# Transformer block on one core: last chunk's sum kept in SBUF, a new order of the turned steps, other queues and banks

## The chip, the core and the metric

The kernel runs on one core of a Trainium2 chip. A core has TensorE (PE) for matrix products, VectorE (DVE), ScalarE (ACT) and GpSimd (POOL) for the rest, and SyncE (SP), which here only issues DMAs. Each engine works through its own list of instructions in order; they meet through semaphores. Matmuls write into the eight banks of PSUM; everything else lives in SBUF or, through DMAs, in device memory. The metric is the time of one execution in microseconds (us).

## The reference

The input is one sequence of 2048 tokens with 448 features. An attention part with 16 heads of width 28, but one common key and one common value head, and an MLP part of width 1792 both read the input, and their results are added to it:

```python
xn = _layernorm(x)
# A: q = (xn @ wq) in 16 heads; k = xn @ wk; v = xn @ wv   (one head each)
#    p = softmax(q k^T * 28**-0.5);  A = (p v) @ wo
# B: y = _layernorm(xn);  B = gelu(y @ w1 + b1) @ w2 + b2
return x + A + B
```

All of it is in float32. The kernel keeps that precision on TensorE by splitting operands into a high and a low part and adding the products.

## The kernel before, in words

**First part (to about 485 us of the trace).** The 2048 tokens are 16 tiles of 128, in four chunks of 512. `acc`, one tile of 16 x 448 per partition, holds x and later x + B. The loads, the normalisation, the q, k and v projections and the split of the weights come first; q goes to device memory (`qd`), k stays in `ks`, v in `vs`. Then the MLP runs in slots, `mlp1` and `mlp2`; at the end of a chunk L537 adds the MLP's result into `acc` and L539 stores that chunk to `ad` in device memory.

**Maxima.** The softmax subtracts each query's true maximum. `max_stream` (L465) computes scores with queries on the partitions (L475, one 128 x 512 block) and takes the maximum of the block on VectorE (L476). Of 800 such blocks most run between the MLP's matmuls, the rest between the steps of the attention. Each head's q comes by four DMAs (`load_m`), two heads ahead. `load_max` transposes a unit's maxima and places them as two further rows of that unit's q, so that the scores come out with the maximum subtracted.

**Attention.** There are 16 units: four chunks of 512 queries times four groups of four heads. A unit has eight steps, each for two tiles of 128 keys; the loop is at L791, with `n` from 0 to 127. `ORDERS` (L28) gives the order of the work within a step as a string, one for units 0 and 1 and one for the "turned" units 2 to 15. The letters:

- `p`: `scores` (L772): two score matmuls (L776) into a tile of two PSUM banks from a pool of two such tiles (`sp`), and one exponential over both (L778), 128 x 1024, into a tile `p` from a ring of seven. A turned step has three of these for three heads, the first two units have four for four heads.
- `P`: `pv` (L709), twice: for each of the two key tiles of the step before, one matmul per head, each in its own 32 columns of TensorE (L714). In a turned step the fourth matmul of a key tile reads the fourth head's tile, which `T` writes.
- `t`: one block of `turned_scores` (L728): the fourth head's scores with queries on the partitions, TensorE L734, then VectorE L735, which copies them to `raw` and keeps their maximum. Every fourth block is followed by a small reduction (L739). This runs eight to ten steps ahead of the unit.
- `x`: `turned_exp` (L745): one wide exponential (L752, 128 x 1024) of half a `raw` tile, and eight DMAs (L756), five by SyncE and three by GpSimd, that rearrange it into the tile `turned`. There are eight of them for a unit.
- `T`: `turn_blocks` (L759): one VectorE block transpose (L761, 128 x 1024) from `turned` into a tile of the ring `p`.
- `m`: one maximum block, if the plan (`weight`, L790) says that one is due. `e`: `load_max` in one step of a unit.
- `n`: one step of `norm_jobs` (L641), which divides a finished unit by its sums. `o`: one step of the output projection (`o_jobs`, L621): twelve matmuls for one tile of 128 tokens, added to rows loaded from `ad` (`load_rows_of`), and the store of the result.

TensorE follows the string strictly, and so does each other engine for its own part. The maximum blocks, the turned score blocks and the output jobs share three PSUM banks (`mtile`). At a unit's start `load_q` fetches the next unit's q. From the start of attention `loads` is GpSimd's queue. In the first steps `prep_wo` (L610) splits the output weights. The last eleven steps (`LEAD`) have no maxima.

The pools of the first part are closed at L585 and L586 and their SBUF is taken over by the attention's tiles, so a tile's first use waits until the last reader of the memory under it has finished.

Of the kernel before, what the change touches and what calls it, by code (L numbers as in the profile page):

```python
# [15 lines left out]
P = 128  # L16
# [10 lines left out]
MLP_MAX = 20  # L27
ORDERS = ("mptmpmtmpmexnPpmonm", "ptpmeoxnPpTtmmnm")  # L28
TURNED = tuple(range(2, 16))
# [7 lines left out]
def block_kernel(ctx, tc, x, wq, wk, wv, wo, w1, b1, w2, b2, out):  # L37
# [21 lines left out]
    qd = [dram.tile([D, S], F32, name=f"qd{i}") for i in range(2)]  # L59

    ks = keep.tile([P, S], F32R, name="ks")
    vs = keep.tile([P, NT, 32], F32, name="vs")
    ident = keep.tile([P, P], F32, name="ident")

    ph1 = ExitStack()
    acc = ph1.enter_context(tc.tile_pool(name="accp", bufs=1)).tile([P, NT, D], F32, name="acc")
    xl_p = ph1.enter_context(tc.tile_pool(name="xl", bufs=2))
# [23 lines left out]
    def load_x(t0, n):  # L91
        nc.sync.dma_start(acc[:, t0:t0 + n, :], xv[:, t0:t0 + n, :])

# [32 lines left out]
    nc.sync.dma_start(b2b, b2[None, :].to_broadcast([P, D]))  # L126
    load_x(2 * CT, 2 * CT)

# [56 lines left out]
    def bn(t):  # L185
        c = t // CT
        if t % CT == 0:
            sts[c] = tmp.tile([P, CT, 6], F32, name="st", bufs=2)
        dve.bn_stats(sts[c][:, t % CT, :], acc[:, t, :])

# [31 lines left out]
    def norm_parts(c, second, first=False, bank=mtile):  # L222
        xh = xt_p.tile([P, 4, CW], F32R, name="xh")
        xl = xl_p.tile([P, 4, CW], F32R, name="xl")
        xts[c, second] = xh, xl
        xns = {}

        def center(k):
            t = CT * c + k
            if first:  # L230
                xn = f(wqp.tile([P, 2, CW], F32R, name="qe", bufs=CT))[:, 0, :]
            else:
                xn = tmp.tile([P, 4 * P], F32, name="xn", bufs=2)
            scale, bias = (lnq, lnqb) if second else (lnr, lnb)
            act.activation(xn[:, 0:D], acc[:, t, :], AF.Identity, bias=bias[:, t:t + 1], scale=scale[:, t:t + 1])
            dve.tensor_scalar(xn[:, D:512], acc[:, t, 384:448], scale[:, t:t + 1], bias[:, t:t + 1],
                              op0=ALU.mult, op1=ALU.add)
# [285 lines left out]
    def mlp2(c, ft, between):  # L523
# [4 lines left out]
        for k in range(CT):  # L528
            ts = slice(k * P, (k + 1) * P)
            pe.matmul(m2[k], hh[:, ts], w2h[:, ft, :], start=(ft == 0), stop=False)  # L530
            yield
            pe.matmul(m2[k], hh[:, ts], w2l[:, ft, :], start=False, stop=False)  # L532
            yield
            pe.matmul(m2[k], hl[:, ts], w2h[:, ft, :], start=False, stop=(ft == NF - 1))  # L534
            if ft == NF - 1:
                a = acc[:, CT * c + k, :]
                dve.tensor_add(a, a, m2[k])  # L537
                if k == CT - 1:
                    nc.sync.dma_start(ad[:, CT * c:CT * c + CT, :], acc[:, CT * c:CT * c + CT, :])  # L539
            if k == 1:  # L540
                between()
            yield
# [26 lines left out]
    for n in range(len(mslots) + 2):  # L569
        c, ft = mslots[n] if n < len(mslots) else (NCH, n - len(mslots))  # L570
        if ft == 12:
            for k in range(CT):
                a = acc[:, CT * c + k, :]
                pool.tensor_add(a, a, b2b)
# [15 lines left out]
    op = ctx.enter_context(tc.tile_pool(name="op", bufs=1, space=PSUM))  # L590

    loads = pool

# [19 lines left out]

    rows = {}

    def load_rows_of(c, tiles):
        for k in tiles:
            rows[c, k] = att.tile([P, D], F32, name="a", bufs=5)
            loads.dma_start(rows[c, k], ad[:, CT * c + k, :])
# [17 lines left out]
    def o_tiles(c, g):  # L637
        ots[c, g] = [att.tile([P, CW], F32R, name=n, bufs=6) for n in ("oth", "otl")]
        return ots[c, g]
# [131 lines left out]

    def scores(u, kt, jobs):  # L772
        s = sp.tile([P, 2, CW], F32, name="s")
        p = pair_of()
        for i, (k, j) in enumerate(jobs):
# [82 lines left out]
```

## Time and profile before

| | us |
|---|---|
| median of three runs | 1160.84 (1159.72 to 1161.23) |
| the profiled execution, time | 1156.78 |
| the profiled execution, span of the trace | 1155.0 |
| score exponentials on ScalarE (L778) | 387.4 in 400 |
| maxima on VectorE (L476) | 526.7 in 800 |
| value matmuls on TensorE (L714) | 246.5 in 2048 records |
| block transposes of the turned head (L761) | 139.2 in 112 |

The table's lower rows are busy times of groups of instructions over the whole span. In rows of the timeline the first two numbers are an instruction's start, counted from the start of the span, and its length, then the engine, the line of the kernel, the operation, and the tiles with their shapes; "x3" stands for three in a row, merged, with one common length. What stands in brackets is how long the engine (PEld for weight loads) was idle before it and what ended that wait. In rows of windows, the stretch is followed by its length, by the busy time (and count) of PE, PEld, DVE, ACT and POOL, by the granted TensorE clock as a share of full speed, the DMA share and GB/s.

### The profile page before, as it was taken

Reading aid. Unit: us, or ns where it says so; the run is one execution under the profiler, and the core shown is the slowest. Engines: PE = TensorE matmul, PEld = TensorE weight load, DVE = VectorE, ACT = ScalarE, POOL = GpSimd, SP = SyncE. Lnnn points to the kernel's source line nnn. Section 1 sums busy time; section 2 is a strip of 40 time slices with the busy share of each in tenths; the row PEclk is TensorE's granted clock in tenths of the full one; section 3 lists DMA queues with packets and bytes.
Section 4 is the critical chain, followed back from the end, with each engine's and each line's share of the span. In section 5 each row is a group of like instructions: output and inputs, shape, how many; then the busy total and the mean of one; then the engine's idle time right before and its main releaser. Section 6 shows DMA issues by size and latency. Waiting matters only on the chain.

```text
span 1155.0 us, 17693 instructions
## 1 busy us (share of the span) xinstructions
PE 1119.7 (97%) x5793; PEld 712.7 (62%) x5793; DVE 914.1 (79%) x1676; ACT 661.1 (57%) x778; POOL 518.9 (45%) x809
## 2 busy tenths in 40 slices
PE   9999999999999999899999999999999999999987
PEld 8778888888888888745444445444445444454443
DVE  7789999999999999857777786677776777766733
ACT  6843322222222111167888887788885888877863
POOL 5333241131113112363547666666774576655530
PEclk9999999999999999989999999999999999999999
DMA  8651101000100102132445576455754565754420
GB/s 279 193 189 54 48 17 56 16 25 16 49 24 16 56 17 55 43 93 66 115 121 151 150 178 159 137 141 150 192 160 127 142 163 137 174 149 136 126 69 32
DMA packets 72359, 121.88 MB, mean 106 GB/s; under 512 B 24862, under 2 KB 33756, under 8 KB 72140
## 3 DMA queue, kind: packets, MB, share of 16 engines
q1 hardware_dynamic: 48076, 73.59, 22.3%
q0 software_dynamic: 22784, 46.59, 15.7%
q8 instruction: 46, 0.75, 0.3%
q10 hardware_dynamic: 1408, 0.57, 0.2%
q14 instruction: 45, 0.37, 0.1%
HBM read 46.11 MB, written 14.79 MB: 53 GB/s over the span
## 4 chain that ended last, share of the span: by engine, by line
PE 67%; ACT 11%; DMA 6%; DVE 6%; issue 3%; POOL 3%; SPq 2%; ACTq 0%; DVEq 0%; POOLq 0%
PE m L475 14%; PE po L714 13%; PE s L776 11%; PE ph L159 9%; ACT p L778 6%; PE m L532 4%; PE m L534 4%; PE m L530 4%; ACT raw L752 3%; DMA turned<-raw 3%; DVE mx L476 2%; SPq L756 2%; POOL turned L756 2%; PE m L734 2%; PE m L628 1%
## 5 line engine op out<-in xcount | busy, mean ns | idle before, releaser
L476 DVE TENSOR_REDUCE mx<-m 128x1 f32<-128x512 f32 x800 | 526.7, 688 | 77.4 <-PE m L475 71.7
L778 ACT ACTIVATE p<-s 128x1024 f32<-128x1024 f32 x400 | 387.4, 1023 | 147.2 <-PE s L776 135.1
L475 PE MATMUL m<-ks,qm 128*128 128x512 f32 x800 | 317.1, 400 | 1.4 <-DVE mx L476 0.6
L776 PE MATMUL s<-xh,ks 128*128 128x512 f32 x800 | 277.5, 430 | 25.6 <-ACT p L778 24.8
L776 PEld LDWEIGHTS s<-xh,ks 128*128 128x128 f32 x800 | 131.3, 189 | 198.5 <-ACT p L778 94.9
L714 PE MATMUL po<-p,vs 128*32 128x512 f32 x2048 | 246.5, 598 | 0.1
L756 POOL DMA_DIRECT2D turned<-raw x336 | 167.7, 506 | 130.3 <-ACT raw L752 120.6
L516 ACT ACTIVATE hr<-ph,b1t 128x512 f32<-128x512 f32 x56 | 38.5, 688 | 305.3 <-PE ph L164 299.3
L521 POOL TENSOR_TENSOR hl<-hr,hh 128x512 fp32r<-128x512 f32 x56 | 72.1, 1288 | 301.9 <-PE m L475 284.6
L735 DVE TENSOR_SCALAR_CACHE_REDUCE raw<-m 128x512 f32<-128x512 f32 x224 | 153.0, 685 | 45.8 <-PE m L734 42.1
L761 DVE STREAM_TRANSPOSE p<-turned 128x1024 f32<-128x1024 f32 x112 | 139.2, 1243 | 48.8 <-PE po L714 21.7
L475 PEld LDWEIGHTS m<-ks,qm 128*128 128x128 f32 x800 | 151.2, 189 | 38.7 <-DVE mx L476 14.1
L714 PEld LDWEIGHTS po<-p,vs 128*32 128x32 f32 x2048 | 53.3, 109 | 121.9 <-issue 120.8
L752 ACT ACTIVATE raw<-raw,m 128x1024 f32<-128x1024 f32 x112 | 126.8, 1145 | 0.0
L734 PE MATMUL m<-ks,q 128*128 128x512 f32 x224 | 88.9, 397 | 0.0
L530 PE MATMUL m<-w2h,hh 128*128 128x448 f32 x224 | 82.5, 368 | 0.0
L534 PE MATMUL m<-w2h,hl 128*128 128x448 f32 x224 | 81.9, 366 | 0.0
L532 PE MATMUL m<-w2l,hh 128*128 128x448 f32 x224 | 81.9, 366 | 0.0
L159 PE MATMUL ph<-xh,w1l 128*128 128x512 f32 x168 | 66.3, 395 | 0.0
L159 PE MATMUL ph<-xl,w1h 128*128 128x512 f32 x168 | 66.2, 394 | 0.0
L159 PE MATMUL ph<-xh,w1h 128*128 128x512 f32 x168 | 66.0, 393 | 0.0
L734 PEld LDWEIGHTS m<-ks,q 128*128 128x128 f32 x224 | 42.0, 188 | 11.0 <-DVE raw L735 1.3
(149 smaller groups left out, 1121.2 us busy)
## 6 DMA issues: line engine op xcount, KB each, us to landing
turned<-raw SPq DMA_DIRECT2D x560, 64.0 KB
turned<-raw POOLq DMA_DIRECT2D x336, 64.0 KB, 2.4
xh<-qd POOLq DMA_DIRECT2D x56, 168.0 KB, 4.4
qm<-qd SPq DMA_DIRECT2D x148, 56.0 KB
qd<-qe SPq DMA_DIRECT2D x24, 256.0 KB
ad<-acc SPq DMA_DIRECT2D x4, 896.0 KB
tr<-ld POOLq DMA_DIRECT2D x56, 64.0 KB, 2.4
a<-ad POOLq DMA_DIRECT2D x16, 224.0 KB, 4.8
```

Of the source, the lines that this page charges most:

```text
L159: pe.matmul(ps, w, v, start=(n == 0), stop=False)
L475: pe.matmul(pm, qm[:, t * P:(t + 1) * P], ks[:, n * CW:(n + 1) * CW], start=True, stop=True)
L476: dve.tensor_reduce(mx[:, CT * j + t, n:n + 1], pm, axis=AX.X, op=ALU.max)
L530: pe.matmul(m2[k], hh[:, ts], w2h[:, ft, :], start=(ft == 0), stop=False)
L714: pe.matmul(po[32 * j:32 * j + 32, :], vs[:, kt, :], ps.pop((u, kt, j)), start=(kt == 0), stop=(kt == NT - 1))
L734: pe.matmul(sc, q3[i][:, t * P:(t + 1) * P], ks[:, n * CW:(n + 1) * CW], start=True, stop=True)
L735: dve.tensor_scalar(raw[:, :, 4 * n:4 * n + 4, :].rearrange("p r b i -> p b r i"), sc.rearrange("p (b r i) -> p b r i", r=4, i=32), SCALE, ...
L752: act.activation(raw[:, rs], raw[:, rs], AF.Exp, bias=m3[:, 4:5], scale=1.0)
L756: q.dma_start(turned[u][32 * r:32 * r + 32, 4 * t + a, :], raw[32 * a:32 * a + 32, r].rearrange("p b i -> p (b i)"))
L761: dve.transpose(p.rearrange("p k (g j) -> p g k j", j=32), turned[u][:, :, 32 * kt:32 * kt + 64].rearrange("p g (k j) -> p g k j", j=32))
L776: pe.matmul(s[:, i], ks[:, (kt + k) * P:(kt + k + 1) * P], qss[u][:, j, :], start=True, stop=True)
L778: act.activation(p, s, AF.Exp, scale=SCALE)
```

## The change

The last chunk of the sum gets a tile of its own (`acc2`) that outlives the first part, is not stored to `ad` and is read in place by the last output jobs; the step that loaded its rows is gone. `acc(t0, n)` and `row(t)` pick the right tile. The x load of chunks 2 and 3 becomes two loads.

`loads` stays SyncE's queue until step 8, then becomes GpSimd's. `prep_wo` moves from steps 2 to 5 to steps 4 to 7. The plan of the maxima gives units 0 and 1 a little less.

In the turned order, one maximum slot stands ahead of the second pair of scores, `T` stands behind the second `t` and the second maximum slot, there are two such slots instead of four, and `x` no longer does two exponentials in the seventh step of a unit. In the last eleven steps the third pair of a step takes two of the three shared banks and two exponentials of half the width instead of one. The rings for rows and for output operands have one buffer less.

```diff
-ORDERS = ("mptmpmtmpmexnPpmonm", "ptpmeoxnPpTtmmnm")
+ORDERS = ("mptmpmtmpmexnPpmonm", "ptmpeoxnPptmTn")
...
+    acc2 = keep.tile([P, CT, D], F32, name="acc2")
...
-    acc = ph1.enter_context(tc.tile_pool(name="accp", bufs=1)).tile([P, NT, D], F32, name="acc")
+    acc1 = ph1.enter_context(tc.tile_pool(name="accp", bufs=1)).tile([P, NT - CT, D], F32, name="acc")
+
+    def acc(t0, n=1):
+        tile_, t0 = (acc1, t0) if t0 < NT - CT else (acc2, t0 - NT + CT)
+        return tile_[:, t0:t0 + n, :]
+
+    def row(t):
+        return acc(t)[:, 0, :]
...
-    load_x(2 * CT, 2 * CT)
+    load_x(2 * CT, CT)
+    load_x(3 * CT, CT)
...
-                if k == CT - 1:
-                    nc.sync.dma_start(ad[:, CT * c:CT * c + CT, :], acc[:, CT * c:CT * c + CT, :])
+                if k == CT - 1 and c < NCH - 1:
+                    nc.sync.dma_start(ad[:, CT * c:CT * c + CT, :], acc(CT * c, CT))
...
-    loads = pool
-
...
-    rows = {}
+    rows = {(NCH - 1, k): acc2[:, k, :] for k in range(CT)}
...
-            rows[c, k] = att.tile([P, D], F32, name="a", bufs=5)
+            rows[c, k] = att.tile([P, D], F32, name="a", bufs=4)
...
-        ots[c, g] = [att.tile([P, CW], F32R, name=n, bufs=6) for n in ("oth", "otl")]
+        ots[c, g] = [att.tile([P, CW], F32R, name=n, bufs=5) for n in ("oth", "otl")]
...
-    def scores(u, kt, jobs):
+    def scores(u, kt, jobs, apart):
+        p = pair_of()
+        if apart:
+            for i, (k, j) in enumerate(jobs):
+                s = mtile([P, CW])
+                pe.matmul(s, ks[:, (kt + k) * P:(kt + k + 1) * P], qss[u][:, j, :], start=True, stop=True)
+                act.activation(p[:, i], s, AF.Exp, scale=SCALE)
+                ps[u, kt + k, j] = p[:, i]
+            return
         s = sp.tile([P, 2, CW], F32, name="s")
-        p = pair_of()
...
-    weight = [0 if n >= len(steps) - LEAD else 24 if u == 0 else 20 if u == 1 else 6 for n, (u, kt) in enumerate(steps)]
+    weight = [0 if n >= len(steps) - LEAD else 24 if n < 6 else 18 if u < 2 else 6 for n, (u, kt) in enumerate(steps)]
...
-        if 2 <= n < 2 + NG:
-            prep_wo(n - 2)
+        if n == 8:
+            loads = pool
+        if 4 <= n < 4 + NG:
+            prep_wo(n - 4)
...
-                scores(u, kt, jobs.pop(0))
+                scores(u, kt, jobs.pop(0), n >= len(steps) - LEAD and len(jobs) == 0)
...
-                if kt == 12:
-                    turned_exp()
...
-                if n == len(steps) - 7:
-                    load_rows_of(NCH - 1, range(CT))
```

More of the change, by code (lines that the diff above doesn't have):

```diff
@@ L91, in load_x @@
     def load_x(t0, n):
-        nc.sync.dma_start(acc[:, t0:t0 + n, :], xv[:, t0:t0 + n, :])
+        nc.sync.dma_start(acc(t0, n), xv[:, t0:t0 + n, :])
     def mtile(shape):
@@ L188, in bn @@
             sts[c] = tmp.tile([P, CT, 6], F32, name="st", bufs=2)
-        dve.bn_stats(sts[c][:, t % CT, :], acc[:, t, :])
+        dve.bn_stats(sts[c][:, t % CT, :], row(t))
     def bn_end(c, k0=0, n=CT):
@@ L234, in center @@
             scale, bias = (lnq, lnqb) if second else (lnr, lnb)
-            act.activation(xn[:, 0:D], acc[:, t, :], AF.Identity, bias=bias[:, t:t + 1], scale=scale[:, t:t + 1])
-            dve.tensor_scalar(xn[:, D:512], acc[:, t, 384:448], scale[:, t:t + 1], bias[:, t:t + 1],
+            act.activation(xn[:, 0:D], row(t), AF.Identity, bias=bias[:, t:t + 1], scale=scale[:, t:t + 1])
+            dve.tensor_scalar(xn[:, D:512], row(t)[:, 384:448], scale[:, t:t + 1], bias[:, t:t + 1],
                               op0=ALU.mult, op1=ALU.add)
@@ L535, in mlp2 @@
             if ft == NF - 1:
-                a = acc[:, CT * c + k, :]
+                a = row(CT * c + k)
                 dve.tensor_add(a, a, m2[k])
-                if k == CT - 1:
-                    nc.sync.dma_start(ad[:, CT * c:CT * c + CT, :], acc[:, CT * c:CT * c + CT, :])
+                if k == CT - 1 and c < NCH - 1:
+                    nc.sync.dma_start(ad[:, CT * c:CT * c + CT, :], acc(CT * c, CT))
             if k == 1:
@@ L572, in block_kernel @@
             for k in range(CT):
-                a = acc[:, CT * c + k, :]
+                a = row(CT * c + k)
                 pool.tensor_add(a, a, b2b)
```

## The prediction

> **What bounds the kernel now.** I read the page first, then the chain of waits for its long stretches, then the timeline of single steps in the turned part, where most attention steps lie.
>
> ```profile
> PE 1119.7 (97%) x5793; PEld 712.7 (62%) x5793; DVE 914.1 (79%) x1676; ACT 661.1 (57%) x778; POOL 518.9 (45%) x809
> ...
> 590.86 1.90 PE po L714 x16
> 709.30 1.85 PE po L714 x16
> 730.53 1.85 PE po L714 x16
> ...
> 1093.25 1.92 PE L714 MATMUL po<-p,vs 128*32 128x512 f32 x16
> ```
>
> TensorE looks full, but a modelled end hides short waits. The other lines are starts of the value block ("P": eight matmuls for two key tiles, once per step). From step 16 (590.86) to step 118 (1093.25) are 102 steps in 502.4 us. Twelve of them carry output-projection jobs: 709.30 to 730.53 is three such steps, 7.08 each, 85.0 for twelve. The other 90 take 417.4, 4.64 each. One of them, in order of time:
>
> ```profile
> 660.44 1.92 PE L714 MATMUL po<-p,vs 128*32 128x512 f32 x16
> 661.61 1.25 DVE L761 STREAM_TRANSPOSE p<-turned 128x1024 f32<-128x1024 f32 x1 [0.37 <-PE po L714]
> 662.30 0.73 PE L776 MATMUL s<-xh,ks 128*128 128x512 f32 x2
> 662.87 0.39 PE L734 MATMUL m<-ks,q 128*128 128x512 f32 x1
> 663.07 2.91 ACT L778 ACTIVATE p<-s 128x1024 f32<-128x1024 f32 x3 [1.72 <-PE s L776]
> 663.10 0.39 PE L475 MATMUL m<-ks,qm 128*128 128x512 f32 x1
> 663.29 0.69 DVE L735 TENSOR_SCALAR_CACHE_REDUCE raw<-m 128x512 f32<-128x512 f32 x1 [0.44 <-PE m L734]
> 664.10 0.68 DVE L476 TENSOR_REDUCE mx<-m 128x1 f32<-128x512 f32 x1
> 664.15 0.73 PE L776 MATMUL s<-xh,ks 128*128 128x512 f32 x2
> 664.71 0.40 PE L475 MATMUL m<-ks,qm 128*128 128x512 f32 x1
> 664.81 0.69 DVE L735 TENSOR_SCALAR_CACHE_REDUCE raw<-m 128x512 f32<-128x512 f32 x1
> 665.04 1.92 PE L714 MATMUL po<-p,vs 128*32 128x512 f32 x16
> 667.89 0.69 DVE L735 TENSOR_SCALAR_CACHE_REDUCE raw<-m 128x512 f32<-128x512 f32 x1 [0.41 <-PE m L734]
> 668.59 0.69 DVE L735 TENSOR_SCALAR_CACHE_REDUCE raw<-m 128x512 f32<-128x512 f32 x1
> ```
>
> The loop that sets 4.60 runs over two engines. P starts at 660.44; the third score pair follows at +1.86 (662.30); ScalarE begins its exponential at 663.07 and needs 2.91/3 = 0.97, to 664.04; only then is the score bank free for the next step's second pair, at 664.15, 1.85 after the third pair; behind that pair stands one maximum (664.71), and P starts 0.89 after the pair. 1.86 + 1.85 + 0.89 = 4.60. VectorE's block transpose "T" (661.61 to 662.86) lies in a hole: VectorE would have waited until 663.29 for the turned scores anyway.
>
> **The turned order: what moves.** Three things change in it. (a) The maximum goes from behind the second pair to ahead of it, into the 0.3 us that TensorE waits there. (b) T goes from behind the third pair to behind the second turned-score block and behind any second maximum. (c) The doubled turned exponential of the seventh step of a unit is spread over two steps.
>
> For (a), the last steps of the kernel, which have no maxima, show the loop without one:
>
> ```profile
> 1106.15 0.73 PE L776 MATMUL s<-xh,ks 128*128 128x512 f32 x2 [0.65 <-ACT p L778]
> 1106.82 1.92 PE L714 MATMUL po<-p,vs 128*32 128x512 f32 x16
> ```
>
> Pair to P is 0.67, so the loop of scores would be 1.86 + 1.85 + 0.67 = 4.38; with two maxima TensorE needs 0.57 + 6 x 0.23 = 1.95 from pair to pair (662.30 to 662.87, then 662.87 to 663.10 for each matmul), so 4.48. Alone this gains about 0.2 a step, and (c) is in that figure.
>
> For (b): the tile that T writes in one step is read by the fourth matmul of P in the next step; the streams of the changed kernel keep that. TensorE is in order, so the second turned-score block cannot start before P has ended: from P's start +2.43 (662.87), VectorE reads it from +2.85 (663.29). That costs VectorE 0.70 (667.89 to 668.59), or 0.81 where the small reduction over four maxima follows (663.29 to 664.10), every other step. A second maximum costs 0.71 (664.10 to 664.81). Then T, 1.25, and a handover: nothing at least, 0.11 at most (the ScalarE end at 664.04 to the matmul at 664.15); I take 0.06. So the next P's fourth matmul can go at 2.85 + 0.70 + 1.25 + 0.06 = 4.86 after P's start, 4.97 with the reduction, and 0.71 later with a second maximum. All are above 4.48, so **T becomes what P waits for**. The head start of the three matmuls ahead of it is worth nothing, since those of T's columns run one after another through the whole of P; if it were worth a quarter of P's 1.86, a step would be 0.46 shorter: the lower bound.
>
> In the changed streams 48 of the 90 plain steps have the second maximum and 45 the reduction: 90 x 4.86 + 45 x 0.11 + 48 x 0.71 = 476.4, against 417.4: **+59.0**. Behind T in VectorE's queue stand the next step's turned scores and maximum; their banks come free later, but each bank asked for before the next P was read ahead of T, so nothing adds up. The twelve steps with output jobs put 7.08 - 4.64 = 2.44 between the second pair and P, which covers T; they gain (a): 12 x (7.08 - 6.87) = **-2.5**.
>
> **Start of attention.** The last chunk's sum no longer leaves SBUF. What that store holds up now:
>
> ```profile
> 480.00:500.00 20.00, 16.49 (x70) 11.98 (x68) 13.75 (x23) 7.06 (x7) 9.58 (x14) 0.83 0.28 91
> 486.42 0.74 PE L776 MATMUL s<-xh,ks 128*128 128x512 f32 x2 [0.56 <-DVE acc L537]
> 490.17 1.94 ACT L778 ACTIVATE p<-s 128x1024 f32<-128x1024 f32 x2 [11.41 <-DMA ad<-acc]
> 491.25 1.22 PE L776 MATMUL s<-xh,ks 128*128 128x512 f32 x2 [2.95 <-ACT p L778]
> 492.70 1.05 PE L776 MATMUL s<-xh,ks 128*128 128x512 f32 x2
> 498.42 1.92 PE L714 MATMUL po<-p,vs 128*32 128x512 f32 x16
> 503.25 0.58 ACT L611 ACTIVATE woh<-turned 128x448 fp32r<-128x448 f32 x1 [1.13 <-DMA turned<-in_A_wo_dram]
> 505.68 1.92 PE L714 MATMUL po<-p,vs 128*32 128x512 f32 x16
> 511.83 1.92 PE L714 MATMUL po<-p,vs 128*32 128x512 f32 x16
> 536.93 1.92 PE L714 MATMUL po<-p,vs 128*32 128x512 f32 x16
> 543.47 1.92 PE L714 MATMUL po<-p,vs 128*32 128x512 f32 x16
> 549.50 1.92 PE L714 MATMUL po<-p,vs 128*32 128x512 f32 x16
> ```
>
> The first exponential's tile overlies memory that the store reads, so it starts at 490.17; free of it, it starts 0.77 after its scores, at 487.2: 3.0 earlier. TensorE then does not sit out 2.95 and keeps its clock (0.83 over that stretch; a pair takes 1.05 instead of 0.73). The eleven maxima of these steps, at 0.68 each from 486.4 on, let the first P go at about 493.8 instead of 498.4. I take **-4.6**, bounds -3.0 and -5.3 (five exponentials of 0.97 and then a pair). Preparing the output weights two steps later removes the 1.13 wait: step 2 (498.42 to 505.68) takes 7.26, step 3 takes 6.15: **-1.1**. Steps 7 and 8 lose one of six maxima, and fall from 6.54 (536.93 to 543.47) to the 6.03 of step 9 (to 549.50), step 6 by about 0.2: **-1.2**. That SyncE issues the loads of the first eight steps is put at nothing: until the turned DMAs start in step 7, its queue has only the output weights besides. Unit 1's loads wait there for a GpSimd clear, with the next heads' loads behind them; those are issued two heads, 32 maxima or five steps, ahead of their use. If that cover were gone, the 3.0 would be lost again. The x load in two parts and one less buffer for rows and outputs I put at nothing, +1 or -1: that x load is under way long before its use, and the fifth buffer is only wanted a unit later. The four row loads that GpSimd no longer issues in step 121 stood on nobody's path.
>
> **Last steps.** The third pair gets banks of its own and two exponentials, so TensorE no longer waits 0.65 at 1106.15.
>
> ```profile
> turned<-raw POOLq DMA_DIRECT2D x336, 64.0 KB, 2.4
> ...
> 1094.27 2.18 ACT L752 ACTIVATE raw<-raw,m 128x1024 f32<-128x1024 f32 x2
> 1111.18 1.92 PE L714 MATMUL po<-p,vs 128*32 128x512 f32 x16
> 1112.21 0.62 ACT L670 ACTIVATE oth<-oc 128x512 fp32r<-128x512 f32 x1
> 1117.37 1.92 PE L714 MATMUL po<-p,vs 128*32 128x512 f32 x16
> 1140.26 1.92 PE L714 MATMUL po<-p,vs 128*32 128x512 f32 x16
> ```
>
> TensorE alone needs 1.86 + 0.57 + 0.46 + 0.67 = 3.56. ScalarE needs 2 x 0.97 + 2 x 0.62 = 3.2, and 4.3 in the two steps that still have a turned exponential (2.18/2). Old, step 118 to 127: 47.0. New: 9 x 3.56 + 4 x 1.8 for the steps with output jobs (6.19 at 1117.37, less 4.37) + 0.7 for ScalarE = 40.0, plus about 2.4, one landing of such a DMA, because the very last turned exponential comes a step later and its DMAs land behind the transpose's turn: 42.4, so **-4.6**, bounds 0 and -7.7.
>
> **Sum.** 59.0 - 2.5 - 4.6 - 1.1 - 1.2 - 4.6 = +45.0. On the profiled execution's own 1156.78 (span 1155.0) this is 1201.8. That execution was 4.1 below the median of the runs, 1160.84; on the median it is **1206**. With the handover between 0 and 0.11 (90 x 0.06 either way) and the bounds above, the forecast's own range is 1190 to 1218.
>
> **Rivals.** *T is hidden after all* (the other side): the late transpose costs nothing, as in the row at 661.61, where VectorE had room. The plain steps fall to 4.38 and 4.48, mean 4.43, plus the 0.04 by which the mean of 4.64 is above the step shown: 90 x (4.47 - 4.64) = -15.3, and -14.0 for the rest: 1132. It decides if T ends within 4.48 of P's start. Against it: the chain 2.43, 2.85, 3.55, 4.80 has no slack before P and each link is a row. 5%.
>
> *The wait costs less*: the head start of P's first matmuls counts, 0.46 off each plain step, -41: 1165, still slower. 6%.
>
> *The gains at both ends fail*: SyncE delivers the first unit late, ScalarE binds the tail; +6.9 and +4.6: 1217. For it: two short exponentials per third pair put more on ScalarE, for which TensorE waits at 1106.15 already. 12%.
>
> *The clock drops*: a late T leaves TensorE idle 0.4 to 1.1 in each step.
>
> ```profile
> 1120.00:1140.00 20.00, 17.40 (x97) 9.52 (x95) 5.60 (x6) 10.06 (x11) 0.00 (x0) 1.00 0.00 0
> ```
>
> At the clock of 492.70 a pair is 1.44 times as long; over the 2.85 of TensorE in the chain that is +1.25 a step, +112: 1318. Against it: 17.40 busy of 20 with 0.65 waits in every step kept the clock at 1.00 here. 3%. The Trainium skill, "TensorE: Matmul & The Clock Gate", section "A second HAM failure mode: psum-queue depth-cycling", says that frequent short idles between groups of matmuls can make the clock swing; by that rule this rival is the outcome, by the row it is not.
>
> **How the numbers follow.** The forecast has 74%. Range: 1186 to 1222, which holds it and the third rival. Changes under 0.2% (2.3 us) could not be told from none. Faster is the first rival, 0.05; no change 0.02, as a part of the second rival that comes out lower still; slower the rest, 0.93.
>
> **What would show it.** Right: plain turned steps alternate between about 4.9 and 5.6 from P to P; VectorE's transpose starts some 3.6 or 4.3 after P's start; the page shows TensorE waiting for VectorE's transpose at the value matmuls, with its busy share down by several points; P of step 1 near 493; last steps near 3.6. Wrong: steps of 4.4 with T done before P (first rival), a clock under 0.95 in the turned part, or step 118 to 127 still taking 47.

## The result, and the profile after

The changed kernel is slower: 1194.46 us (median of four runs, 1193.25 to 1195.62) against 1160.5 for the kernel before on the same chip, a ratio of 1.0293 (95% interval 1.0275 to 1.031). Its profiled execution has a span of 1193.9 us, the kernel before's 1155.0, so the two traces differ by 38.9 us.

In the changed file the value matmul is L722 (before: L714), a turned score block L742 and L743 (L734, L735), the transpose T L769 (L761), the pair of scores and its exponential L791 and L793 (L776, L778), a maximum L485 and L486 (L475, L476).

First the page of the changed kernel: busy times, the chain of waits by engine, and the group of value matmuls (busy, mean ns, idle before).

```profile
PE 1175.4 (98%) x5793; PEld 725.9 (61%) x5793; DVE 896.0 (75%) x1676; ACT 667.4 (56%) x789; POOL 505.1 (42%) x779
...
PE 86%; DVE 7%; DMA 2%; ACT 2%; issue 1%; SPq 0%; POOL 0%; DVEq 0%; ACTq 0%; POOLq 0%
...
L722 PE MATMUL po<-p,vs 128*32 128x512 f32 x2048 | 314.0, 600 | 2.7 <-DVE p L769 2.7
```

TensorE seems fuller than before, 98% against 97%, with the same 5793 matmuls. What grew is the value matmuls, from 246.5 us to 314.0: a block that has begun and then waits inside is counted as busy. The page alone would suggest that TensorE is the bound; the views of waits and of time say otherwise. The waits of the turned part, each with its sum, count and longest:

```profile
DVE raw L743 <- PE m L742: 175.4, 102, 2.6
...
PEld po L722 <- DVE p L769: 54.5, 86, 1.3
```

The value block's weight loads waited 54.5 us for the transpose, in 86 places, a wait that this view of the kernel before doesn't list. VectorE meanwhile waited 175.4 us for turned score blocks, four times as long as before:

```profile
DVE raw L735 <- PE m L734: 42.1, 93, 0.5
```

Two engines that wait for each other by turns are a loop. Here are two of its steps, in order of time, in the changed kernel:

```profile
694.49 0.73 PE L791 MATMUL s<-xh,ks 128*128 128x512 f32 x2
695.49 0.69 DVE L743 TENSOR_SCALAR_CACHE_REDUCE raw<-m 128x512 f32<-128x512 f32 x1 [1.70 <-PE m L742]
696.30 1.23 DVE L769 STREAM_TRANSPOSE p<-turned 128x1024 f32<-128x1024 f32 x1
697.00 2.49 PE L722 MATMUL po<-p,vs 128*32 128x512 f32 x16
697.59 0.14 PEld L722 LDWEIGHTS po<-p,vs 128*32 128x32 f32 x5 [0.44 <-DVE p L769]
699.42 0.74 PE L791 MATMUL s<-xh,ks 128*128 128x512 f32 x2
700.43 0.69 DVE L743 TENSOR_SCALAR_CACHE_REDUCE raw<-m 128x512 f32<-128x512 f32 x1 [1.70 <-PE m L742]
701.04 0.69 DVE L486 TENSOR_REDUCE mx<-m 128x1 f32<-128x512 f32 x1
701.65 1.24 DVE L769 STREAM_TRANSPOSE p<-turned 128x1024 f32<-128x1024 f32 x1
702.08 2.77 PE L722 MATMUL po<-p,vs 128*32 128x512 f32 x16
702.94 0.16 PEld L722 LDWEIGHTS po<-p,vs 128*32 128x32 f32 x8 [0.71 <-DVE p L769]
704.77 0.73 PE L791 MATMUL s<-xh,ks 128*128 128x512 f32 x2
```

The value block starts at 697.00, but its fourth matmul goes only at 697.59, when T has ended; the third pair follows 1.83 later (699.42), VectorE takes up the second turned block 1.01 after that (700.43), a maximum at 701.04, T at 701.65, and the next fourth matmul goes at 702.94, 0.05 after T's end. 1.83 + 1.01 + 1.22 + 1.24 + 0.05 = 5.35 from one fourth matmul to the next. The step before it, with the reduction but without the second maximum, took 699.42 - 694.49 = 4.93.

The trace adds up as follows. A step is counted from the start of one value block to the start of the next and bears the number of the block that ends it, as in the prediction; the twelve "job steps" are those with output jobs.

| stretch | before | after | difference | predicted |
|---|---|---|---|---|
| up to the block of step 16 | 590.79 | 582.76 | -8.0 | -6.9 |
| 90 plain steps of 16 to 118 | 417.4 | 464.2 | +46.8 | +59.0 |
| 12 job steps | 85.0 | 89.9 | +4.9 | -2.5 |
| step 118 to 128 | 49.5 | 44.6 | -4.9 | -4.6 |

With 0.2 behind step 128 that is the 38.9, but for rounding. Plain steps alternate in some units between 4.88 and 5.40, in others between 5.07 and 5.20.

### The profile page after: what moved, and what is told of

Its sections match the earlier page's. It is cut to its first block, busy times and chain, and to the rows that moved or that the text cites. A ratio compares the mean times of both kernels' runs of the same rounds, so it can differ in the third digit from the quotient of the medians.

```text
span 1193.9 us, 17703 instructions
## 1 busy us (share of the span) xinstructions
PE 1175.4 (98%) x5793; PEld 725.9 (61%) x5793; DVE 896.0 (75%) x1676; ACT 667.4 (56%) x789; POOL 505.1 (42%) x779
## 4 chain that ended last, share of the span: by engine, by line
PE 86%; DVE 7%; DMA 2%; ACT 2%; issue 1%; SPq 0%; POOL 0%; DVEq 0%; ACTq 0%; POOLq 0%
PE po L722 24%; PE s L791 16%; PE m L485 15%; PE ph L169 9%; PE m L742 4%; PE m L542 4%; PE m L544 4%; PE m L540 4%; DVE mx L486 2%; DMA xh<-qd 1%; PE m L636 1%; PE ph L172 1%; PE ph L174 1%; PE m L638 1%; PE m L637 1%
## 5 line engine op out<-in xcount | busy, mean ns | idle before, releaser
L486 DVE TENSOR_REDUCE mx<-m 128x1 f32<-128x512 f32 x800 | 526.6, 688 | 49.1 <-PE m L485 43.5
L793 ACT ACTIVATE p<-s 128x1024 f32<-128x1024 f32 x389 | 382.2, 1026 | 159.3 <-PE s L791 158.5
L485 PE MATMUL m<-ks,qm 128*128 128x512 f32 x800 | 321.6, 405 | 1.3 <-DVE mx L486 0.6
L722 PE MATMUL po<-p,vs 128*32 128x512 f32 x2048 | 314.0, 600 | 2.7 <-DVE p L769 2.7
L743 DVE TENSOR_SCALAR_CACHE_REDUCE raw<-m 128x512 f32<-128x512 f32 x224 | 150.5, 672 | 177.6 <-PE m L742 175.4
L791 PE MATMUL s<-xh,ks 128*128 128x512 f32 x778 | 260.9, 419 | 1.7 <-ACT p L793 0.8
L791 PEld LDWEIGHTS s<-xh,ks 128*128 128x128 f32 x778 | 131.8, 188 | 140.3 <-ACT raw L760 68.8
L485 PEld LDWEIGHTS m<-ks,qm 128*128 128x128 f32 x800 | 150.2, 188 | 52.8 <-DVE raw L743 16.7
L722 PEld LDWEIGHTS po<-p,vs 128*32 128x32 f32 x2048 | 68.2, 108 | 177.0 <-issue 116.2
L769 DVE STREAM_TRANSPOSE p<-turned 128x1024 f32<-128x1024 f32 x112 | 138.5, 1237 | 18.0 <-PE po L722 9.4
L760 ACT ACTIVATE raw<-raw,m 128x1024 f32<-128x1024 f32 x112 | 127.5, 1139 | 0.0
L742 PE MATMUL m<-ks,q 128*128 128x512 f32 x224 | 88.5, 395 | 0.0
L742 PEld LDWEIGHTS m<-ks,q 128*128 128x128 f32 x224 | 42.1, 188 | 10.6 <-DVE raw L743 0.6
```

The costliest lines, as they stand in the source:

```text
L485: pe.matmul(pm, qm[:, t * P:(t + 1) * P], ks[:, n * CW:(n + 1) * CW], start=True, stop=True)
L486: dve.tensor_reduce(mx[:, CT * j + t, n:n + 1], pm, axis=AX.X, op=ALU.max)
L722: pe.matmul(po[32 * j:32 * j + 32, :], vs[:, kt, :], ps.pop((u, kt, j)), start=(kt == 0), stop=(kt == NT - 1))
L742: pe.matmul(sc, q3[i][:, t * P:(t + 1) * P], ks[:, n * CW:(n + 1) * CW], start=True, stop=True)
L743: dve.tensor_scalar(raw[:, :, 4 * n:4 * n + 4, :].rearrange("p r b i -> p b r i"), sc.rearrange("p (b r i) -> p b r i", r=4, i=32), SCALE, ...
L769: dve.transpose(p.rearrange("p k (g j) -> p g k j", j=32), turned[u][:, :, 32 * kt:32 * kt + 64].rearrange("p g (k j) -> p g k j", j=32))
```

## The experiments

Twelve kernels were run, each beside the kernel before on the same chip. Where an edit is to "the changed kernel", its diff is against that. The times by stretch, from the profiled execution of each, with the mean over the plain steps and, apart, over the 20 of them that open a unit (those that end with its first or second value block):

| kernel | median | block 16 | 90 plain steps (mean) | 20 that open a unit, mean | 12 job steps | 118 to 128 |
|---|---|---|---|---|---|---|
| before | 1160.5 | 590.79 | 417.4 (4.64) | 4.59 | 85.0 | 49.5 |
| after | 1194.5 | 582.76 | 464.2 (5.16) | 5.34 | 89.9 | 44.6 |
| e1_t_early | 1174.2 | 582.62 | 434.4 (4.83) | 6.17 | 100.8 | 43.3 |
| e2_t_early_double | 1142.2 | 582.67 | 413.5 (4.59) | 4.88 | 87.9 | 42.8 |
| e3_t_late_in_before | 1207.2 | 594.35 | 459.1 (5.10) | 5.13 | 90.3 | 50.1 |
| e4_t_before_second_max | 1188.8 | 582.84 | 447.5 (4.97) | 5.35 | 100.9 | 44.5 |
| e5_max_behind | 1147.1 | 583.29 | 419.1 (4.66) | 4.73 | 87.8 | 42.9 |
| e6_lead3 | 1124.7 | 583.08 | 401.0 (4.46) | 4.45 | 85.3 | 40.9 |
| e7_tail_shared | 1201.3 | 583.13 | 466.5 (5.18) | 5.42 | 89.8 | 49.7 |
| e8_sum_kept_in_before | 1154.7 | 589.43 | 417.3 (4.64) | 4.59 | 85.8 | 49.6 |
| e9_before_max_lead3 | 1179.0 | 583.29 | 443.4 (4.93) | 5.13 | 96.0 | 40.9 |
| e10_late_lead3 | 1193.0 | 583.06 | 463.8 (5.15) | 5.31 | 90.0 | 40.9 |
| e11_loads_pool | 1194.1 | 582.83 | 463.6 (5.15) | 5.31 | 89.9 | 44.5 |
| e12_max_behind_lead3 | 1138.2 | 583.56 | 413.0 (4.59) | 4.59 | 86.6 | 40.9 |

**The late transpose alone, added to the kernel before.** If the place of T is the cause, it must do the same harm without the rest of the change.

```diff
-ORDERS = ("mptmpmtmpmexnPpmonm", "ptpmeoxnPpTtmmnm")
+ORDERS = ("mptmpmtmpmexnPpmonm", "ptpmeoxnPptmTmnm")
```

> The kernel before with only the transpose moved behind the second turned-score block and one maximum slot (turned order ptpmeoxnPptmTmnm). Theory: plain steps go from 4.64 to about 5.15 and the output steps lengthen a little, so 1160.5 + 47 + 5 = about 1212 (1203 to 1220). Rivals 1 and 2: within 5 us of 1160.5, as neither the maximum nor the exponential has moved.

1207.16 us, ratio 1.04 (1.0385 to 1.0416), inside the range. The plain steps grew by 41.7, the job steps by 5.3; the 3.6 more up to step 16 are the first steps' wait for the output weights, which the edit doesn't touch. The timeline of that kernel, with VectorE and the value block:

```profile
663.66 0.69 DVE L735 TENSOR_SCALAR_CACHE_REDUCE raw<-m 128x512 f32<-128x512 f32 x1 [1.70 <-PE m L734]
664.47 0.68 DVE L476 TENSOR_REDUCE mx<-m 128x1 f32<-128x512 f32 x1
665.07 1.23 DVE L761 STREAM_TRANSPOSE p<-turned 128x1024 f32<-128x1024 f32 x1
665.40 2.85 PE L714 MATMUL po<-p,vs 128*32 128x512 f32 x16
666.35 0.16 PEld L714 LDWEIGHTS po<-p,vs 128*32 128x32 f32 x8 [0.80 <-DVE p L761]
```

The same links as above, and the same wait inside the block. One letter of the order string carries the loss.

**The transpose early again, in the changed kernel.** The counterpart: take that letter back and keep all else.

```diff
-ORDERS = ("mptmpmtmpmexnPpmonm", "ptmpeoxnPptmTn")
+ORDERS = ("mptmpmtmpmexnPpmonm", "ptmpeoxnPpTtmn")
```

> The changed kernel with the block transpose back right behind the third pair of scores (turned order ptmpeoxnPpTtmn); all else as changed. Theory (the late transpose sets the step): plain turned steps fall from 5.16 to about 4.45, no wait of the value matmuls on the transpose inside a unit; the first transpose of a unit may wait for the last exponential's DMAs, 0 to 1.6 us a unit, so 1130 to 1153. Rival 1 (the maximum ahead of the second pair holds TensorE up through the banks): still about 1194. Rival 2 (the single exponential per step, not the transpose's place, makes the fourth head late): 1180 to 1194.

1174.23 us (1165.39 to 1176.16), ratio 1.0096 (1.0068 to 1.0124), above the 1153 that was the upper end. Inside the units the steps fell to 4.37 and 4.50, as the theory has it, but the two opening steps of a unit took up to 9.4 and 7.4. In order of time, where one unit ends and the next begins:

```profile
614.87 1.14 ACT L760 ACTIVATE raw<-raw,m 128x1024 f32<-128x1024 f32 x1
621.56 0.40 PE L742 MATMUL m<-ks,q 128*128 128x512 f32 x1
623.83 1.25 DVE L769 STREAM_TRANSPOSE p<-turned 128x1024 f32<-128x1024 f32 x1 [4.31 <-DMA qm<-qd]
625.00 0.65 DVE L743 TENSOR_SCALAR_CACHE_REDUCE raw<-m 128x512 f32<-128x512 f32 x1
625.72 0.50 PE L485 MATMUL m<-ks,qm 128*128 128x512 f32 x1 [3.77 <-DVE raw L743]
```

A unit's turned scores are complete only three steps before its first T, so its last exponential comes in the step just before that T. Here it is the sixteenth L760 of the trace, which ends at 616.01 (614.87 + 1.14). T needs all that its DMAs bring. SyncE issues the last of them at 618.50; by the trace's semaphore record it lands at 623.16, and T starts at 623.83, 7.82 after the exponential. T stands ahead of the next turned block on VectorE, TensorE needs that block's bank back, and so sits 3.77 us. (The view puts the wait down to another DMA, `qm<-qd`, none of which has landed before 625.45; the five waits that name `xh<-qd` and four that name `turned<-raw` are of the same place and size.) In that stretch GpSimd also issues eight loads of q, and between 618.50 and 623.83 the DMA engines are 0.82 busy; how much of the landing's 4.7 us is due to that, no run separates. Of the old order, this change had removed what made up for it: the doubled exponential in the seventh step, which had a unit's last exponential done a step earlier.

Part of this kernel's time is the clock. Its granted clock is 0.983 over the profiled execution and 0.991 and 0.992 in the two that took 1165, against 0.999 in e6 below. By estimate that is at most 0.016 x 1173.5 = 19 us of the 49.5 between the two.

**With the doubled exponential back.**

```diff
...
+                if kt == 12:
+                    turned_exp()
```

> As the run before, and the two exponentials in the seventh step of a unit are back. Theory: 1130 to 1137; if the run before had its units' first steps stretched by late DMAs, that stretch is gone here, otherwise the two are alike and this one loses about 0.3 a unit (4 us) to the doubled exponential. Rival 2: the whole loss of 34 us goes only here. Rival 1: still about 1194.

1142.2 us, ratio 0.9846 (0.9829 to 0.9862), 5 above the upper end of what was expected: the opening steps fell from 6.17 to 4.88, not to 4.5, since some units still wait for a landing (step 97 took 8.29). (The order string is that of e1.)

**The turned scores and exponentials one step earlier.** The same landing, hidden in another way: e1 with a lead of three steps instead of two.

```diff
-ORDERS = ("mptmpmtmpmexnPpmonm", "ptmpeoxnPptmTn")
+ORDERS = ("mptmpmtmpmexnPpmonm", "ptmpeoxnPpTtmn")
...
-                if n >= 8 * (TURNED[0] - 1) - 2:
+                if n >= 8 * (TURNED[0] - 1) - 3:
```

> As e1 (transpose early, one exponential in every step), but the turned scores start one step earlier, so that a unit's last exponential lies two steps ahead of its first transpose. Theory: steps of 4.43 inside the units and no stretched first steps: before's 1160.5 - 8.0 (start) - 6.7 (end) - 18 (turned part) = about 1128 (1121 to 1135), the fastest of all. Rival (something else than the DMAs of the last exponential stretches the first steps of a unit, such as the next unit's loads on GpSimd): 1142 to 1174, as e2 or e1.

1124.71 us, ratio 0.9695 (0.967 to 0.9719): inside the range, and faster than both kernels. The same unit as in e1, from its last exponential:

```profile
610.79 1.14 ACT L760 ACTIVATE raw<-raw,m 128x1024 f32<-128x1024 f32 x1
...
619.80 1.25 DVE L769 STREAM_TRANSPOSE p<-turned 128x1024 f32<-128x1024 f32 x1 [0.67 <-ACT p L793]
...
622.89 0.68 DVE L743 TENSOR_SCALAR_CACHE_REDUCE raw<-m 128x512 f32<-128x512 f32 x1
623.13 1.93 PE L722 MATMUL po<-p,vs 128*32 128x512 f32 x16
623.49 0.68 DVE L486 TENSOR_REDUCE mx<-m 128x1 f32<-128x512 f32 x1
624.23 1.25 DVE L769 STREAM_TRANSPOSE p<-turned 128x1024 f32<-128x1024 f32 x1
```

The last DMA of that exponential, issued at 614.41, lands at 616.91, 2.9 ahead of T, which waits for no DMA (the 0.67 ends with an exponential). The value block takes its 1.93, and the loop of scores sets the step: 4.37 to 4.50, where the prediction had 4.38 and 4.48 for that loop.

**Is the late T's loss in truth a landing?** The earlier lead alone, with T left late.

```diff
-                if n >= 8 * (TURNED[0] - 1) - 2:
+                if n >= 8 * (TURNED[0] - 1) - 3:
```

> The changed kernel (transpose late) with the turned scores one step earlier. Theory (inside the units the chain through the late transpose sets the step, whatever the DMAs do): steps stay at 5.1 to 5.2, only a few long steps and the 2.4 at the end go: 1190 (1185 to 1193). Rival (the DMAs of the single exponential are the main cause of the changed kernel's loss): 1160 or less.

1192.95 us, ratio 1.0288 (1.0268 to 1.0309), at the upper end of the range. The plain steps didn't move (5.15); only the stretch from step 118 to 128 lost 3.7. Of this, 2.5 is the landing of the kernel's very last turned exponential (3.45 for 5.96 in the step that it stalled), and 1.2 comes of the last T that stands behind turned blocks, which is now a step earlier (the step behind block 118 takes 3.45 for 4.69). With e1 and e6 this makes all four pairings of T's place and the lead: the lead is worth 1.5 us while T is late, and 50 once it is early.

**The transpose late, but ahead of the second maximum.** Only the maximum is taken out of the chain.

```diff
-ORDERS = ("mptmpmtmpmexnPpmonm", "ptmpeoxnPptmTn")
+ORDERS = ("mptmpmtmpmexnPpmonm", "ptmpeoxnPptTmn")
```

> The changed kernel with the transpose one place earlier, ahead of the second maximum but still behind the second turned-score block (turned order ptmpeoxnPptTmn). Theory: the 48 plain steps with a second maximum lose the 0.6 that it puts ahead of the transpose, so steps of 4.9 to 5.0 throughout, 1194.5 - 48 x 0.55 = about 1168 (1162 to 1175). Rivals: unchanged at about 1194, since the TensorE stream is the same.

1188.83 us, ratio 1.0248 (1.0224 to 1.0272), above the range. The steps inside units fell from 5.11 to 4.86 (mean of 70), as the chain has it, but the opening steps stayed at 5.35 and the job steps grew by 11.0. With the landing hidden (e4 with the lead of three):

> As e4 (transpose behind the second turned-score block, ahead of the second maximum) with the turned scores one step earlier, as in e6. Theory (two loops: the chain through the transpose inside a unit, and the DMAs of the last exponential at a unit's start): the stretched first steps of e4 go, the inner steps stay at 4.8 to 4.9, so the turned part takes 90 x 4.84 + 85 = 521 instead of e4's 548 and the end loses its 2.4: about 1159 (1154 to 1165). Rival (the transpose's place has a price of its own that the chain does not hold): 1185.

1178.96 us, ratio 1.0172 (1.0149 to 1.0195), again above the range. The job steps came down by 4.9 and the opening ones by 0.2 each. Of the ten units without output jobs, each still has one step of 5.4 to 5.7, and five have one of 5.97 to 6.12 besides. One of the latter (from block 18 to block 19), in order of time:

```profile
596.24 0.39 PE L485 MATMUL m<-ks,qm 128*128 128x512 f32 x1
597.25 1.23 DVE L769 STREAM_TRANSPOSE p<-turned 128x1024 f32<-128x1024 f32 x1
598.41 0.65 DVE L486 TENSOR_REDUCE mx<-m 128x1 f32<-128x512 f32 x1
599.12 0.28 PE L468 MATMUL m<-ident,mr 128*12 128x128 f32 x1 [0.96 <-DVE mx L486]
599.32 1.92 PE L722 MATMUL po<-p,vs 128*32 128x512 f32 x16
```

`load_max` (L468) takes one of the three shared banks, and its turn falls on the bank that the maximum block of 596.24 fills and that VectorE reads only behind T. So TensorE waits 0.96 ahead of the value block. (It isn't the maximum itself that is needed: those of the unit that is being loaded were complete before 240 us.) Both experiments were priced by the steady steps alone; whose bank the moved maximum holds was left out. How much of the 6.1 this wait makes, and what stretches the steps of 5.4 to 5.7, was not tried by a run of its own.

**The maximum ahead of the second pair.** Putting it back behind the pair, first in e2 and then in e6. The diff shows the order string alone, against the changed kernel; the rest is as in those two.

```diff
-ORDERS = ("mptmpmtmpmexnPpmonm", "ptmpeoxnPpTtmn")
+ORDERS = ("mptmpmtmpmexnPpmonm", "ptpmeoxnPpTtmn")
```

> As e2 (transpose early, doubled exponential), but the maximum stands behind the second pair again (turned order ptpmeoxnPpTtmn). Theory (the faster steps of e2 are given back at the units' starts, where the transpose waits for the DMAs of the last turned exponential): steps inside a unit go from 4.43 back to 4.6, the units' first steps are no longer stretched, and the time stays within 5 us of e2's 1142. Rival (the maximum's place is a net gain of 0.17 a step): 1142 + 15 = 1157.

> As e6 (transpose early, turned scores one step earlier), but with the first maximum slot behind the second pair of scores again, as in the kernel before. Only the place of that maximum differs from e6. Theory (the maximum ahead of the second pair takes about 0.18 us out of the loop of scores in every plain step, 4.64 against 4.46, and this was mostly hidden in e2 and e5 by the stretched first steps of each unit): 90 x 0.18 = 16 us more than e6's 1124.7, so 1138 to 1144, inner steps 4.64. Rival (the place of the maximum is worth only the 5 us by which e5 and e2 differ, the rest of e6's gain is the landing): 1127 to 1132.

In e2's company it cost 4.9 (1147.11 us, ratio 0.9894, 0.987 to 0.9919), in e6's 13.5 (1138.24 us, ratio 0.9811, 0.9791 to 0.9832), both inside their ranges. The second is the clean figure: 4.59 against 4.46 in the plain steps, 12.0 over 90, and 1.3 over the job steps. In e2 the opening steps were stretched by a landing in any case (4.88; 4.73 in e5), which hid much of it.

**The banks of the last steps.** The third pair in the shared pool, with one exponential, as before:

```diff
-                scores(u, kt, jobs.pop(0), n >= len(steps) - LEAD and len(jobs) == 0)
+                scores(u, kt, jobs.pop(0), False)
```

> The changed kernel, but the third pair of the last eleven steps shares the two-bank tiles and has one exponential again. Theory: those steps go from 3.45 back to about 4.37, so +5 us: 1199.5 (1198 to 1201), ratio to before about 1.034. Rival (the end gained because the row loads are gone): 1194.5.

1201.26 us, ratio 1.0356 (1.0331 to 1.0381), a hair above the range: step 118 to 128 takes 5.1 longer, as expected. The other 1.7 of the 6.8 between the medians has its like in the plain steps (+2.3 from profile to profile, most of it in opening steps), which the edit doesn't touch.

**The last chunk's sum, kept in SBUF, in the kernel before.** `acc2`, its readers and the missing store and loads, with the split load of x and the smaller rings; nothing else of the change.

```diff
+    acc2 = keep.tile([P, CT, D], F32, name="acc2")
...
-                if k == CT - 1:
-                    nc.sync.dma_start(ad[:, CT * c:CT * c + CT, :], acc[:, CT * c:CT * c + CT, :])
+                if k == CT - 1 and c < NCH - 1:
+                    nc.sync.dma_start(ad[:, CT * c:CT * c + CT, :], acc(CT * c, CT))
...
-                if n == len(steps) - 7:
-                    load_rows_of(NCH - 1, range(CT))
```

> The kernel before with only the sum of the last chunk kept in SBUF (and with it the split x load and the smaller rings). Theory: the first value block comes at about 493.8 instead of 498.4, and the wait on the output weights goes too, 1160.5 - 4.6 - 1 = about 1155 (1153 to 1157). Rival (the gain at the start is SyncE's loads): 1160.

1154.73 us, ratio 0.9957 (0.9937 to 0.9976), inside the range. The first value block starts at 494.02 instead of 498.42, as expected, but the expectation's second half was wrong, so that the total is right in part by luck: the wait for the output weights stays, and steps 2 and 3 take 8.65 and 7.78.

```profile
500.24 0.58 ACT L621 ACTIVATE woh<-turned 128x448 fp32r<-128x448 f32 x1 [2.51 <-DMA turned<-in_A_wo_dram]
```

That wait is absent only in the kernels with the later `prep_wo`, which this one doesn't have.

**Loads by GpSimd from the start**, as before, in the changed kernel:

```diff
+    loads = pool
+
...
-        if n == 8:
-            loads = pool
```

> The changed kernel with GpSimd issuing the first unit's loads again. Theory (the start gains by the sum kept in SBUF and by the later split of the output weights, not by the queue): first value block within 0.5 of 493.8 and the time within 2 of 1194.5. Rival (the queue is worth something): steps 2 to 8 longer, 1196 to 1200.

1194.13 us, ratio 1.0296 (1.0271 to 1.032), first value block at 493.92, as expected: the queue is worth nothing here.

## Why the prediction was right, and where its sizes were off

**The cause.** The forecast named T as what P waits for, through P, the third pair, the second turned block, the second maximum and T. The trace shows that chain link by link, and e3 and e6 show it from both sides: T's place alone costs the kernel before 46.8 us (1207.16 against 1160.37 on the same chip), and without it, with the landing hidden, the changed kernel would be at 1124.7. The rival "T is hidden after all" falls, and so does "the wait costs less": the first three matmuls of the block do start before T, but the third pair comes 1.83 after the fourth matmul in both steps shown (697.59 to 699.42, 702.94 to 704.77), as if the whole block had waited.

**The size of the plain steps: +46.8 for +59.0.** The mis-sized term is what VectorE needs from the second turned block to T: 0.70, and 0.71 more for a second maximum. The trace has four kinds of plain step; the step here is from one fourth matmul of the value block (its weight load) to the next, the typical value of each kind:

| second maximum | reduction | steps | predicted | measured | second turned block to T, predicted | measured |
|---|---|---|---|---|---|---|
| no | no | 22 | 4.86 | 4.75 | 0.70 | 0.62 |
| no | yes | 21 | 4.97 | 4.93 | 0.81 | 0.81 |
| yes | no | 23 | 5.57 | 5.35 | 1.41 | 1.22 |
| yes | yes | 24 | 5.68 | 5.53 | 1.52 | 1.41 |

The last two columns make 22 x 0.08 + 23 x 0.19 + 24 x 0.11 = 8.8 of the 12.2. The other links are together 0.03 a step shorter (2.84 for 2.85, T 1.24 for 1.25, the handover 0.05 for 0.06), 2.7 in all, and there is one second maximum fewer than the 48 that were counted, 0.7.

Why the term came out too long: both spacings that it was read from held more than the operation. At 668.59 VectorE had waited for TensorE, whose matmul of 668.16 ends at 668.56. At 664.81 it hadn't, since that matmul ended at 664.18, but there its list has seven waits on semaphores that the timeline leaves out. The trace of before has a pair without either, a maximum directly behind a turned block:

```profile
664.81 0.69 DVE L735 TENSOR_SCALAR_CACHE_REDUCE raw<-m 128x512 f32<-128x512 f32 x1
...
665.43 0.69 DVE L476 TENSOR_REDUCE mx<-m 128x1 f32<-128x512 f32 x1
```

0.62 from one to the other, and as much from a turned block to T in the changed kernel:

```profile
658.47 0.69 DVE L743 TENSOR_SCALAR_CACHE_REDUCE raw<-m 128x512 f32<-128x512 f32 x1 [1.70 <-PE m L742]
...
659.09 1.24 DVE L769 STREAM_TRANSPOSE p<-turned 128x1024 f32<-128x1024 f32 x1
```

Two things outside the chain nearly cancel. The plain step behind each group of job steps starts with a block whose T was ready, and takes 4.37 to 4.51; opening steps in which T starts late take up to 5.90. What holds T up there was not tried apart; it isn't the landing, since e10 has the same opening steps (5.31).

**Job steps: +4.9 for -2.5.** Here a step of the prediction failed: that each bank asked for before the next P was read ahead of T, so that nothing adds up. In order of time, in the changed kernel:

```profile
725.66 1.24 DVE L769 STREAM_TRANSPOSE p<-turned 128x1024 f32<-128x1024 f32 x1
726.00 0.28 PE L468 MATMUL m<-ident,mr 128*12 128x128 f32 x1
726.82 0.21 DVE L666 RECIPROCAL rc<-rc 128x16 f32<-128x16 f32 x1
726.95 0.63 DVE L743 TENSOR_SCALAR_CACHE_REDUCE raw<-m 128x512 f32<-128x512 f32 x1
727.64 0.47 PE L636 MATMUL m<-woh,oth 128*128 128x448 f32 x1 [1.37 <-DVE raw L743]
```

In these steps `load_max` (L468) takes one of the three shared banks as well. So the output job behind it gets the bank of the turned block that VectorE reads behind T, at 726.95, and not that of the maximum read ahead of T, at 725.06; TensorE waits 1.37 ahead of the job. The three steps of this kind (43, 75, 107) take 8.70, 8.10 and 8.70, where before took 7.13, 7.13 and 7.14: +4.1. The three that enter a group carry the wait inside the block (7.51, 7.83, 7.51 for 7.04, 7.26, 7.03): +1.5. The other six gained 0.7 between them, by the maximum's place as predicted, though less.

**Start of attention: -8.0 for -6.9.** The first value block was predicted at 493.8 and came at 493.82; ScalarE starts 0.82 after its scores (486.94 to 487.76), and the clock stays at 1.00:

```profile
480.00:500.00 20.00, 19.39 (x94) 12.84 (x96) 17.32 (x30) 10.25 (x11) 4.27 (x4) 1.00 0.47 111
```

e8 shows that the kept sum does this without the rest of the change. The wait for the output weights was worth 2.1, not 1.1: steps 2 and 3 take 5.58 and 5.71, for 7.26 and 6.15. Its size differs by execution: 13.4 for the two steps in the profile of before, 16.4 in e8, 18.2 in e3, which has the same code there. Steps 6 to 8 gained 0.5, not 1.2, and steps 9 to 16 another 0.9. That the other queue is worth nothing, e11 shows; the split load and the smaller rings weren't tried apart.

**Last steps: -4.9 for -4.6.** e7 confirms 5.1 for the banks. The landing of the last turned exponential appears as predicted, in one stalled value block:

```profile
1148.43 1.06 PE L722 MATMUL po<-p,vs 128*32 128x512 f32 x6
1149.68 1.25 DVE L769 STREAM_TRANSPOSE p<-turned 128x1024 f32<-128x1024 f32 x1 [5.73 <-ACT p L793]
1150.97 1.90 PE L722 MATMUL po<-p,vs 128*32 128x512 f32 x10 [1.48 <-DVE p L769]
```

The block starts at 1148.43 and goes on at 1150.97; the next starts 5.97 after it instead of 3.45. That is 2.5 for the 2.4 predicted, and e10, where the landing is hidden, has 3.45 there. The 0.7 that was set aside for ScalarE isn't seen as such; in its place the step behind block 118 takes 4.69, since its block still waits 1.12 for the last T behind turned blocks.

**The sum.** 46.8 + 4.9 - 8.0 - 4.9 + 0.2 = 39.0 from profile to profile (38.9 by the spans), where +45.0 was forecast. The medians differ by less, 34.0: the profiled execution of before lies 3.7 under its median, that of after 1.2 over its own. The short wait for output weights in that one profile of before may be part of it; no run here separates it.

That the total lies in the range is partly luck. The plain steps were put 12.2 too high and the job steps 7.4 too low, and the two offset each other. And the lower end of 1190 isn't what the bounds named beside it give: from 1206, less 5.4 for the handover, 0.7 for the start, 3.1 for the last steps and 1 for the load of x, it is 1196, above the measured 1194.5. The mechanism and its direction owe nothing to this.

**Signs that were named.** Steps alternating, the value matmuls waiting for T, first block near 493, last steps near 3.6 (3.45): all there. T starts 3.5 to 4.25 after the fourth matmul, as forecast, but 4.4 to 4.7 after the block's start, since the block starts ahead of T. One was wrong: TensorE's busy share was to fall by several points, and rose by one, because a block waiting inside is counted as busy. The rival of a falling clock didn't occur: over the stretch from 582 to 1137, waits of up to 1.3 us in nearly every step left it at 1.00.

```profile
582.00:1137.00 555.00, 550.02 (x2764) 251.30 (x2767) 362.84 (x759) 415.21 (x436) 321.32 (x581) 1.00 0.53 137
```

So the rule of the Trainium skill named beside that rival ("TensorE: Matmul & The Clock Gate", section "A second HAM failure mode: psum-queue depth-cycling") was not borne out at this depth of waiting.

**What the change would have been worth without the late T.** e6 against after: 63.2 in the plain steps, 4.6 in the job steps, 3.7 in the last ones. Against the kernel before, e6's span of 1122.6 is 32.4 shorter: 16.2 in the plain and job steps (502.5 less 486.3), of which the maximum's place makes 13.2 by e12 (499.5 there), 7.7 up to step 16 and 8.6 from step 118 on. What is left of the 16.2 is, for the most part, the evenly spread turned exponential: before, the seventh step of a unit took some 4.87 and the others 4.6; in e12 it takes 4.59.

## What to carry to other kernels

When an operation is moved later on an engine that has room, don't ask whether that engine has room; follow the loop from its consumer back to its own inputs through every in-order queue, and compare its length with the loop that sets the step now. Follow every shared buffer in that loop too: which bank an operation gets decides whom it waits for. When such a move is taken back, ask what its lateness had been hiding: here one letter was worth 70 us, but only together with transfers that started a step earlier; taken back alone it gave 20. And read a duration from two instructions that stand back to back with no wait between them, or the sum counts waiting as work.

## What the runs showed that was not expected

- Four matmuls in column groups of 32 behaved as one block: with the fourth operand late by 0.71, the block took 2.77 instead of 1.92. The pair behind it came 1.83 after the fourth matmul; where nothing is late it comes 1.86 after the block's start (660.44 to 662.30 in the kernel before). So nothing was gained by the three that went ahead.
- The clock of TensorE bore many short waits, and mostly not a long one. Of nine idles of 1.9 to 4.3 us at the openings of units in e1, seven come with a spell at half clock that lasts 3.4 or 6.8 us, and two don't (1.90, ending at 754.48, and 3.42, ending at 1047.66). After the 3.77 us shown above the granted clock was 0.57 for the next 4 us:

```profile
626.00:630.00 4.00, 4.00 (x19) 0.91 (x18) 2.44 (x5) 2.06 (x2) 0.98 (x3) 0.57 0.16 26
```

- The last rearranging DMA of a unit took 4.7 us to land in e1 (618.50 to 623.16), with DMA busy at 0.82 until T began, and 2.5 in e6 (614.41 to 616.91), with 0.52 between 614.41 and 619.80. The page's median, for those that GpSimd issues, is 2.3 to 2.4.
